# Spectrum sums on GpSimd beside VectorE products that read PSUM, with third buffers and an earlier start of loads and transposes

## The chip, the cores and the metric

One core of a Trainium2 chip. The metric is the device time of the whole kernel in microseconds (us). Most executions of one kernel agree within 0.3%, so differences below about 0.5 us are read with care. "Span" is the profiled time from the first to the last instruction, 1.8 us less than the timed run of the same execution (211.5 of 213.35 us for before).

## The reference, cut to what matters

```python
def _A_ref(x, w_r, w_i):                       # x: (1, 2048, 640) bf16
    X = rfft2(x.astype(float32))
    X = X * (w_r + 1j * w_i)                   # the filter: w_r, w_i (2048, 321)
    return irfft2(X, s=(2048, 640)).astype(bfloat16)

def _B_ref(x, w_gate, w_up, w_down):           # (640,1536), (640,1536), (1536,640)
    return ((x @ w_gate) * (x @ w_up)) @ w_down

xn = layernorm(x)
out = x + _A_ref(xn, w_r, w_i) + _B_ref(xn, w_gate, w_up, w_down)
```

The two branches share the normalised input. The Fourier branch is done as matmuls with small tables and radix-5 butterflies on VectorE. In the middle it has 16 filter steps. Each takes a part of the spectrum from PSUM, multiplies it by the weights, and forms sums of the products. These sums are what the change moves.

## The kernel before

The kernel gives every piece of work to a list scheduler of its own, written in Python, as a task with an engine, an assumed duration, the buffers it reads and writes, and a priority. The scheduler fixes one order for each engine before the kernel is built. Each engine's queue is written in that order. So a change of a duration, of a buffer or of an engine re-plans everything that comes after it.

The loads at the start and the statistics of the normalisation:

```python
dma("ld_sm", V("SM"), d_sm.rearrange("p t n -> p (t n)"), 128 * 768, [(b_sm, None)], prio=0.002, q="act")
# ... (cut)
for gi, (b0, nb) in enumerate(_X_LOADS):
    dma("ld_x%d" % gi, v_x[:, b0:b0 + nb, :], xv[:, b0:b0 + nb, :], 128 * nb * 1280,
        [(b_x, ("s", b0, b0 + nb))], prio=(0.0, 0.01, 0.02, 0.03, 0.042, 0.06)[gi])
# ... (cut) for each row block b below 8:
def em_bn(c, b=b):
    c.e.bn_stats(v_st[:, b, 0:6], v_x[:, b, 0:320])
    return c.e.bn_stats(v_st[:, b, 6:12], v_x[:, b, 320:640])
T("bn%d" % b, "dve", 800.0, em_bn, reads=[(b_x, ("s", b, b + 1))], writes=[(b_st, ("b", b, b + 1))], prio=pbase)
```

Row blocks 0 to 3 of the normalised x are transposed on TensorE (tasks `T0_b`), the others by DMA transposes on the queue of SyncE (L816). Then follow the gate/up units (`GU_ft_b`, L951: TensorE, evicted by ScalarE at L709, multiplied on VectorE at L966).

A filter step:

```python
for t in range(16):
    r2 = t % 2
    # ... (cut: four loads of filter rows; D: matmuls, L994; C: matmuls into a pair of PSUM banks, L1015-L1018)
    def em_wm(c, tc=tc, r2=r2, wr=wr):         # products: PSUM times weights in SBUF
        for h in range(2):
            for w in range(2):
                c.e.tensor_tensor(v_p[:, r2, w, :, 128*h:128*h+128], xh, wv[:, w], _OP.mult)    # L1030, cut
        return c.e.tensor_tensor(v_p[:, r2, :, :, 256:321], ps[:, bk:bk + 2, 256:321], ...)     # L1033, cut
    def em_cb(c, r2=r2):                       # sums: two SBUF inputs each
        p00, p01, p10, p11 = (v_p[:, r2, 0, 0], v_p[:, r2, 0, 1], v_p[:, r2, 1, 0], v_p[:, r2, 1, 1])
        c.e.tensor_tensor(v_y[:, r2, 512:768], p01[:, 0:256], p10[:, 0:256], _OP.add)           # L1045
        c.e.scalar_tensor_tensor(v_y[:, r2, 896:961], p01[:, 256:321], -1.0, p10[:, 256:321], _OP.mult,
                                 _OP.subtract)                                                  # L1046
        c.e.tensor_tensor(v_y[:, r2, 768:833], p00[:, 256:321], p11[:, 256:321], _OP.subtract)  # L1048
        return c.e.tensor_tensor(v_y[:, r2, 256:512], p00[:, 0:256], p11[:, 0:256], _OP.subtract)  # L1049
    T("CB_%d" % t, "dve", 2 * _d_dve(256) + 2 * _d_dve(65), em_cb, ...)
    # ... (cut: NG on ScalarE copies and negates, L1054-L1056; IA: inverse matmuls, L1070/L1071)
```

After it come the inverse stage (matmuls L1099, butterflies on VectorE L1121 to L1154) and the down-projection (L1172 and L1180), whose result is added by VectorE (L1187).

Of the kernel before, what the change touches and what calls it, by code (L numbers as in the profile page):

```python
# [15 lines left out]
_DMA_LAT = 1000.0  # L16
_DMA_ISSUE = 440.0
# [489 lines left out]
_LP = 321  # L507
_SN = math.sin(2.0 * math.pi / 5.0)
# [4 lines left out]
def _d_mm(n):  # L513
    return max(n, 64) / 2.4 + 2.5


def _d_dve(n):
    return n * 1.04 + 65.0


def _d_dve_psum(n):
    return n * 1.04 + 70.0
# [14 lines left out]
def _d_act(n):  # L537
    return n * 0.833 + 80.0
# [8 lines left out]
def _build(nc, A_x, A_w_r, A_w_i, B_w_gate, B_w_up, B_w_down, out, opts=None):  # L547
# [3 lines left out]
    with es:  # L551
# [8 lines left out]
        sch.caps = {"glu": opts.get("cap_glu", 2), "acc": opts.get("cap_acc", 4), "fill": 1}  # L560
        lay = {}
# [43 lines left out]
        b_p = alloc("P", 2 * 4 * 2 * _LP)  # L605
        b_y = alloc("Y", 2 * 1024)
        o_end = max(o_end, cur[0])
        cur[0] = o_3
        b_tc = alloc("TC", 2 * 2560)
        b_vt = alloc("VT", 2 * 2048)  # L610
# [12 lines left out]
        def V(name):  # L623
            off, sz = lay[name]
            return arena[:, off: off + sz]
# [29 lines left out]
        v_p = V("P").bitcast(_F32).rearrange("p (r w c l) -> p r w c l", r=2, w=2, c=2)  # L655
        v_y = V("Y").rearrange("p (r n) -> p r n", r=2)
        v_tc = V("TC").bitcast(_F32).rearrange("p (r s u n) -> p r s u n", r=2, s=5, u=2)
# [54 lines left out]
        dma("ld_sm", V("SM"), d_sm.rearrange("p t n -> p (t n)"), 128 * 768, [(b_sm, None)], prio=0.002, q="act")  # L712
# [34 lines left out]
        for gi, (b0, nb) in enumerate(_X_LOADS):  # L747
            dma("ld_x%d" % gi, v_x[:, b0:b0 + nb, :], xv[:, b0:b0 + nb, :], 128 * nb * 1280,
                [(b_x, ("s", b0, b0 + nb))], prio=(0.0, 0.01, 0.02, 0.03, 0.042, 0.06)[gi])
        muls = {}  # L750
        for gi, (b0, nb) in enumerate(_LN_GROUPS):
            pbase = 1.0 + 0.05 * gi if gi < 4 else opts.get("ln_prio", 5.99) + 0.05 * (gi - opts.get("ln_lead", 3))
            for b in range(b0, b0 + nb):
# [13 lines left out]
                else:  # L767
                    def em_bn(c, b=b):
                        c.e.bn_stats(v_st[:, b, 0:6], v_x[:, b, 0:320])  # L769
                        return c.e.bn_stats(v_st[:, b, 6:12], v_x[:, b, 320:640])  # L770
                    T("bn%d" % b, "dve", 800.0, em_bn, reads=[(b_x, ("s", b, b + 1))],
                      writes=[(b_st, ("b", b, b + 1))], prio=pbase)
# [3 lines left out]
                    T("ag%d" % b, "dve", 130.0, em_ag, reads=[(b_st, ("b", b, b + 1))],  # L776
                      writes=[(b_mv, ("b", b, b + 1))], prio=pbase)
            if b0 >= opts.get("act_stats", 8):
# [3 lines left out]
                T("mb%d" % b0, "dve", 160.0, em_mb, reads=[(b_m32, ("b", b0, b0 + nb)), (b_ss, ("b", b0, b0 + nb))],  # L782
# [6 lines left out]
            T("ve_%d" % gi, "dve", 80.0, em_ve, reads=[(b_mv, gk)], writes=[(b_ve, gk)], prio=pbase - 0.006)  # L789
# [3 lines left out]
            T("sd_%d" % gi, "act", 120.0, em_sd, reads=[(b_ve, gk)], writes=[(b_sd, gk)], prio=pbase - 0.006)  # L793
# [3 lines left out]
            T("rs_%d" % gi, "dve", 80.0, em_rs, reads=[(b_sd, gk)], writes=[(b_rs, gk)], prio=pbase)  # L797

            for b in range(b0, b0 + nb):
# [4 lines left out]
                T("sub%d" % b, "dve", 290.0, em_sub, reads=[(b_mv, ("b", b, b + 1))],  # L804
# [6 lines left out]
                muls[b] = T("mul%d" % b, ("dve", "act") if b >= 4 else "dve", {"dve": 290.0, "act": _d_act(640) + 93}, em_mul, reads=[(b_rs, ("b", b, b + 1))],  # L811
                  writes=[(b_x, ("s", b, b + 1))], prio=pb)

                if b >= opts.get("xt_dma", 4):
                    def em_xt(c, b=b):
                        return c.e.dma_start_transpose(v_xt[:, :, b * 128:(b + 1) * 128], v_x[:, b, :])  # L816
                    T("xt%d" % b, "sp", opts.get("xt_issue", 1500.0), em_xt, reads=[(b_x, ("s", b, b + 1))],
# [13 lines left out]
                t0 = T("T0_%d" % b, "pe", 5 * _d_mm(128), em_t0, reads=[(b_x, ("s", b, b + 1)), (b_sm, None)],  # L831
                       prio=pb, bank="pair" if b < opts.get("e0_split", 2) else "single", cls="a")

                if b < opts.get("e0_split", 2):
# [9 lines left out]
                    hold(t0, es_)  # L844
                    continue
# [10 lines left out]
        for g in range(8):  # L856
# [46 lines left out]
            for u in range(2):  # L903
                def em_r(c, gr=gr, u=u):
                    bk = bank_of(c.t)
                    ins = None
                    for k, (f, o) in enumerate(((0, 1), (1, 0), (1, 1), (0, 0), (2, 0))):
# [8 lines left out]
                       reads=[(b_f, ("r", 3 * gr, 3 * gr + 3)), (b_sm, None)], prio=pf, bank="pair", cls="a")  # L916
# [19 lines left out]
        for ui, (at_, ci, ft0) in enumerate(units):  # L936
# [6 lines left out]
            for u in range(2):  # L943
# [10 lines left out]
                gu = T("GU_%d_%d" % (ft, b0), "pe", 10 * _d_mm(n), em_gu,  # L954
# [322 lines left out]
```

## Time and profile before

| | before |
|---|---|
| time, median of 4 runs beside the changed kernel | 212.87 us (212.59 to 213.29) |
| span | 211.5 us |
| VectorE busy | 185.1 us |
| GpSimd busy | 0.2 us |
| first transpose on TensorE | 5.88 us |
| matmuls that start late | 8.2 us |

All matmuls from the first transpose on, back to back, would take 194.6 us. What the distances between their starts exceed that by is summed by stretch of the span and called **late matmuls**. First transpose + 194.6 + late matmuls + 2.7 for the last output gives the span.

### The profile page before, as it was taken

Reading aid. Unit: us, or ns where it says so; the run is one execution under the profiler, and the core shown is the slowest. Engines: PE = TensorE matmul, PEld = TensorE weight load, DVE = VectorE, ACT = ScalarE, POOL = GpSimd, SP = SyncE. Lnnn points to the kernel's source line nnn. Section 1 sums busy time; section 2 is a strip of 40 time slices with the busy share of each in tenths; the row PEclk is TensorE's granted clock in tenths of the full one; section 3 lists DMA queues with packets and bytes.
Section 4 is the critical chain, followed back from the end, with each engine's and each line's share of the span. In section 5 each row is a group of like instructions: output and inputs, shape, how many; then the busy total and the mean of one; then the engine's idle time right before and its main releaser. Section 6 shows DMA issues by size and latency. Waiting matters only on the chain.

```text
span 211.5 us, 5204 instructions
## 1 busy us (share of the span) xinstructions
PE 202.6 (96%) x2044; PEld 169.4 (80%) x2044; DVE 185.1 (87%) x536; ACT 122.1 (58%) x281; POOL 0.2 (0%) x4
## 2 busy tenths in 40 slices
PE   8799999799999999989999999999999899999994
PEld 7699899688898998978888898898766677667773
DVE  3699989899999989389999999948999999999821
ACT  2375899799866666878999897776222202200000
POOL 0000000000000000000000000000000000000000
PEclk9999999999999999999999999999999999999999
DMA  6999999531133000002224233025042223222411
GB/s 190 304 341 395 384 299 218 104 62 31 34 64 65 0 3 0 0 18 56 56 58 120 55 62 90 3 62 155 3 121 82 64 63 108 81 77 65 126 47 47
DMA packets 30456, 21.74 MB, mean 103 GB/s; under 512 B 10336, under 2 KB 29408, under 8 KB 30304
## 3 DMA queue, kind: packets, MB, share of 16 engines
q1 hardware_dynamic: 28320, 20.34, 35.6%
q10 hardware_dynamic: 2112, 1.08, 1.9%
q8 instruction: 16, 0.26, 0.5%
q14 instruction: 8, 0.07, 0.1%
HBM read 16.82 MB, written 2.62 MB: 92 GB/s over the span
## 4 chain that ended last, share of the span: by engine, by line
PE 67%; DVE 22%; DMA 6%; issue 3%; ACT 1%; SPq 0%; DVEq 0%
PE ps L951 41%; PE ps L1172 12%; DMA arena<-arena 3%; DMA arena<-in_A_x_dram 2%; PE ps L1070 2%; PE ps L1071 2%; DVE arena L1187 2%; PE ps L994 2%; PE ps L912 2%; DVE arena L1144 1%; DVE arena L1145 1%; DVE arena L1153 1%; DVE arena L1137 1%; PE ps L1015 1%; ACT arena L709 1%
## 5 line engine op out<-in xcount | busy, mean ns | idle before, releaser
L709 ACT ACTIVATE arena<-ps 128x512 bf16<-128x512 f32 (+5 forms) x189 | 99.9, 572 | 55.0 <-PE ps L1099 28.2
L951 PE MATMUL ps<-arena 128*128 128x256 bf16 (+1 forms) x1080 | 112.8, 261 | 2.8 <-DMA arena<-arena 1.2
L951 PEld LDWEIGHTS ps<-arena 128*128 128x128 bf16 x1080 | 93.6, 98 | 14.2 <-ACT arena L709 1.6
L1172 PE MATMUL ps<-arena 128*128 128x320 bf16 x384 | 56.5, 299 | 0.3 <-DVE arena L1187 0.3
L1172 PEld LDWEIGHTS ps<-arena 128*128 128x128 bf16 x384 | 37.2, 98 | 14.7 <-DVE arena L1187 0.7
L966 DVE TENSOR_TENSOR arena<-arena 128x512 bf16<-128x512 bf16 (+1 forms) x54 | 21.1, 390 | 10.5 <-ACT arena L709 10.4
L1030 DVE TENSOR_TENSOR arena<-ps,arena 128x256 f32<-128x256 f32 x64 | 22.6, 414 | 0.0
L1187 DVE TENSOR_TENSOR arena<-ps,arena 128x320 bf16<-128x320 f32 x32 | 15.4, 482 | 6.7 <-PE ps L1180 6.7
L1071 PE MATMUL ps<-arena 128*128 128x128 bf16 x80 | 10.7, 219 | 0.0
L1070 PE MATMUL ps<-arena 128*128 128x128 bf16 x80 | 10.6, 219 | 0.0
L1180 PE MATMUL ps<-arena 128*128 128x320 bf16 x32 | 9.1, 300 | 0.5 <-DVE arena L1154 0.4
L1070 PEld LDWEIGHTS ps<-arena 128*128 128x128 bf16 x80 | 8.7, 112 | 0.5
L865 DVE TENSOR_TENSOR arena<-arena 128x384 f32<-128x384 bf16 x16 | 8.8, 550 | 0.0
L1071 PEld LDWEIGHTS ps<-arena 128*128 128x128 bf16 x80 | 8.7, 112 | 0.1
L769 DVE BATCH_NORM_STATS2 arena<-arena 128x6 f32<-128x320 bf16 x8 | 3.9, 489 | 3.8 <-DMA arena<-in_A_x_dram 3.7
L1033 DVE TENSOR_TENSOR arena<-ps,arena 128x260 f32<-128x260 f32 x16 | 7.1, 441 | 0.0
L1045 DVE TENSOR_TENSOR arena<-arena 128x256 bf16<-128x256 f32 x16 | 6.7, 421 | 0.2
L1054 ACT ACTIVATE arena<-arena 128x256 bf16<-128x256 bf16 x16 | 6.6, 414 | 0.3 <-DVE arena L1049 0.2
L1049 DVE TENSOR_TENSOR arena<-arena 128x256 bf16<-128x256 f32 x16 | 6.7, 418 | 0.0
L866 DVE TENSOR_TENSOR arena<-arena 128x256 f32<-128x256 bf16 x16 | 6.7, 417 | 0.0
L1152 DVE TENSOR_TENSOR arena<-arena 128x640 bf16<-128x640 f32 x8 | 6.5, 818 | 0.1
L762 ACT ACTIVATE arena<-arena 128x640 bf16<-128x640 bf16 x8 | 6.6, 828 | 0.0
(71 smaller groups left out, 212.2 us busy)
## 6 DMA issues: line engine op xcount, KB each, us to landing
arena<-in_A_x_dram SPq DMA_DIRECT2D x20, 160.0 KB, 2.6
out_dram<-arena SPq DMA_DIRECT2D x32, 80.0 KB, 1.6
arena<-c_tf SPq DMA_DIRECT2D x4, 384.0 KB, 11.8
arena<-in_A_w_r_dram SPq DMA_DIRECT2D x32, 40.1 KB, 2.4
arena<-in_A_w_i_dram SPq DMA_DIRECT2D x32, 40.1 KB, 2.2
arena<-in_B_w_gate_dram SPq DMA_DIRECT2D x4, 320.0 KB, 7.9
arena<-in_A_x_dram SPq DMA_DIRECT2D x1, 1280.0 KB, 12.1
arena<-c_ti SPq DMA_DIRECT2D x2, 512.0 KB, 14.5
```

What stands on the lines that cost most here:

```text
L709: return c.e.activation(dst, src, _ACTF.Copy)
L865: c.e.tensor_tensor(uo[:, o, :, 0:3, :], v_xb[:, b:b + 2, 0:6:2, :], v_xb[:, b:b + 2, 5:10:2, :], op)
L866: ins = c.e.tensor_tensor(uo[:, o, :, 3:5, :], v_xb[:, b:b + 2, 6:10:2, :], v_xb[:, b:b + 2, 1:5:2, :], op)
L951: ins = c.e.matmul(ps[:, bk, w * n:(w + 1) * n], v_gw[:, w, j, ft, :], v_xt[:, j, rows], start=(j == 0), stop=(j == 4))
L966: return c.e.tensor_tensor(v_ht[:, ft0:ft0 + 2, rows], v_gbf[:, rr, :, 0:n], v_gbf[:, rr, :, n:2 * n], _OP.mult)
L1030: c.e.tensor_tensor(v_p[:, r2, w, :, 128 * h:128 * h + 128].rearrange("p c (m k) -> p c m k", k=4), xh.rearrange("p c (m k) -> p c m k", k ...
L1033: ins = c.e.tensor_tensor(v_p[:, r2, :, :, 256:321], ps[:, bk:bk + 2, 256:321].unsqueeze(1).to_broadcast([128, 2, 2, 65]), v_w[:, wr, :, 0 ...
L1070: c.e.matmul(dst, l1, v_ti[:, t, 0, :], start=True, stop=False)
L1071: ins = c.e.matmul(dst, l2, v_ti[:, t, 1, :], start=False, stop=True)
L1172: ins = c.e.matmul(ps[:, bk, 0:320], v_ht[:, ft, a * 128:(a + 1) * 128], v_wd[:, ft, sl3], start=(ft == 7), stop=False)
L1180: return c.e.matmul(ps[:, bank_of(ag2), 0:320], v_sm[:, 2, :], v_v[:, a, sl3], start=False, stop=True)
L1187: return c.e.tensor_tensor(v_out[:, a % 2, sl3], ps[:, bk, 0:320], v_xr[:, xs, sl3], _OP.add)
```

## The change

The intent: VectorE is full in the filter stage and busy for 87% of the span, GpSimd idle. The products read PSUM, to which GpSimd has no access by the page that the prediction cites, so they stay on VectorE, and the two long sums of each step go to GpSimd. The two short sums stay on VectorE. Third buffers are to hide the longer latency. Independently of that, the start and the order of the loads are changed, the scheduler's assumed durations are set anew, and at most two tasks of class `a`, those of the spectrum among them, may hold PSUM banks at once (the cap). The core of the diff:

```diff
-_DMA_LAT = 1000.0
-_DMA_ISSUE = 440.0
+_DMA_LAT = 1300.0
+_DMA_ISSUE = 520.0
 def _d_dve(n):
-    return n * 1.04 + 65.0
+    return n * 1.04 + 72.0
 # (cut: the other durations likewise, e.g. DMA transposes 1500 -> 1100)
         sch.caps = {"glu": ..., "acc": ..., "fill": 1}
+        if opts.get("cap_a", 2):
+            sch.caps["a"] = opts.get("cap_a", 2)
-        b_p = alloc("P", 2 * 4 * 2 * _LP)
-        b_y = alloc("Y", 2 * 1024)
+        b_p = alloc("P", 3 * 4 * 2 * _LP)
+        b_y = alloc("Y", 2 * _YS)
+        b_y3 = alloc("Y3", _YS, at=lay["STAT"][0])
+        b_tc3 = alloc("TC3", 2560, at=lay["GBF"][0])
-        dma("ld_sm", V("SM"), ..., prio=0.002, q="act")
+        dma("ld_sm0", v_sm[:, 0, :], ..., prio=0.002, q="act")
+        dma("ld_sm1", v_sm[:, 1:3, :], ..., prio=0.25)
-                [(b_x, ("s", b0, b0 + nb))], prio=(0.0, 0.01, 0.02, 0.03, 0.042, 0.06)[gi])
+                [(b_x, ("s", b0, b0 + nb))], prio=(0.0, 0.003, 0.02, 0.03, 0.042, 0.06)[gi])
-                    T("bn%d" % b, "dve", 800.0, em_bn, ...)          # both halves in one task
+                        bns.append(T("bn%d_%d" % (b, i), "dve", 420.0, em_bn, ...))
+                    if b == 1:
+                        bns[0].deps.add(muls[0])
+                        bns[1].deps.add(e0_first)                     # behind the first copy from PSUM
-                        64 * 642, ..., after=[wpad])                   # filter rows
+                        64 * 642, ..., after=[wpad, muls[opts.get("w_after", 15)]])
 # (cut: the same "after" for the inverse tables and the down weights)
-            def em_cb(c, r2=r2):
+            def em_cb(c, ar=ar):
+                c.e.tensor_tensor(v_y[ar][:, 512:768], p01[:, 0:256], p10[:, 0:256], _OP.add)
+                return c.e.tensor_tensor(v_y[ar][:, 256:512], p00[:, 0:256], p11[:, 0:256], _OP.subtract)
+            ce = opts.get("cb_eng", "pool")
+            T("CB_%d" % t, ce, {"dve": 2 * _d_dve(256), "pool": opts.get("cb_pool", 1600.0)}, em_cb, ...)
+            def em_cd(c, ar=ar):
                 # (the two sums of 65 columns, as before)
+            T("CD_%d" % t, "dve", 2 * _d_dve(65), em_cd, ...)
-        sch.affinity = opts.get("affinity", 600.0)
+        sch.affinity = opts.get("affinity", 1500.0)
```

## The prediction

> **What bounds the kernel now.** I read the page first, then the sum of waits, then the timeline of TensorE, VectorE and the DMA queue where the waits point, then the windows by stage.
>
> ```profile
> span 211.5 us, 5204 instructions
> PE 202.6 (96%) x2044; PEld 169.4 (80%) x2044; DVE 185.1 (87%) x536; ACT 122.1 (58%) x281; POOL 0.2 (0%) x4
> ...
> PE   8799999799999999989999999999999899999994
> DVE  3699989899999989389999999948999999999821
> ```
>
> TensorE is busy for 96% of the span, VectorE for 87%, and GpSimd does nothing. Busy TensorE is not proof of a full pace, so I summed in the trace the distances between the starts of successive matmuls. Back to back, a matmul of 128 columns takes 55.9 ns, of 256 columns 109, of 320 columns 135.7, of 321 columns 137. The first transpose starts at 5.88 us; all matmuls from there, back to back, would take 194.6 us; the output after the last one takes 2.7 us. That makes 5.9 + 194.6 + 2.7 = 203.2 of the 211.5 us. The other **8.2 us** are matmuls that started late, and they are all that this change can win: it removes no matmul. The lost time by place: 1.3 us before 10 us, 0.8 from 10 to 30, 1.5 from 30 to 40, 1.0 from 40 to 55, 0.8 at 91.6, 2.75 between 157 and 189. From 60 to 90 and from 93 to 155 nothing is lost.
>
> The three places that matter, as the timeline shows them:
>
> ```profile
> 8.16 1.05 PE L951 MATMUL ps<-arena 128*128 128x128 bf16 x16 [0.95 <-DVE arena L775]
> ...
> 6.87 0.49 DVE L769 BATCH_NORM_STATS2 arena<-arena 128x6 f32<-128x320 bf16 x1 [1.14 <-DMA arena<-in_A_x_dram]
> 7.28 0.48 DVE L770 BATCH_NORM_STATS2 arena<-arena 128x6 f32<-128x320 bf16 x1
> 7.68 0.34 DVE L710 COPY arena<-ps 128x384 bf16<-128x384 bf16 x1
> ...
> 39.07 6.91 PE L951 MATMUL ps<-arena 128*128 128x256 bf16 x60 [1.21 <-DMA arena<-arena]
> ...
> 32.16 7.94 SPq L816 DMA_TRANSPOSE arena<-arena  x4
> ...
> 158.11 0.45 PE L1180 MATMUL ps<-arena 128*128 128x320 bf16 x2 [0.41 <-DVE arena L1154]
> 160.61 0.72 PE L1099 MATMUL ps<-arena 128*128 128x128 bf16 x10 [0.29 <-DVE arena L1131]
> ```
>
> At 8.16 us the first gate matmuls start: their transposed input sat in PSUM from about 6.3 us, but VectorE waited for the second row block of x (landed at 6.85), did both its statistics, and only then the copy. At 39.07 TensorE waits for DMA transposes whose input was normalised by 25.7 us; they were issued from 32.16 on, because sixteen filter loads and others, at 0.6 us of queue each, stood before them. After 157 us TensorE waits for VectorE's last butterflies (L1121 to L1154).
>
> ```profile
> 105.02 0.41 DVE L1045 TENSOR_TENSOR arena<-arena 128x256 bf16<-128x256 f32 x1
> 105.35 0.22 DVE L1046 SCALAR_TENSOR_TENSOR arena<-arena 128x65 bf16<-128x65 f32 x1
> 105.49 0.22 DVE L1048 TENSOR_TENSOR arena<-arena 128x65 bf16<-128x65 f32 x1
> 105.62 0.42 DVE L1049 TENSOR_TENSOR arena<-arena 128x256 bf16<-128x256 f32 x1
> 105.96 1.41 DVE L1030 TENSOR_TENSOR arena<-ps,arena 128x256 f32<-128x256 f32 x4
> ...
> 92.00:138.00 46.00, 45.56 (x503) 40.26 (x504) 45.16 (x149) 39.90 (x109) 0.00 (x0) 1.00 0.25 59
> ```
>
> This is one of the 16 filter steps, and the window over them all (TensorE, its weight loads, VectorE, ScalarE, GpSimd): VectorE is full (45.2 of 46 us), yet TensorE loses only 0.6 us, since gate/up matmuls fill its time. So VectorE sets the pace of the filter steps, but not the time there; it sets when the last butterflies can begin.
>
> **What the Trainium skill says.** "GPSIMD Engine Reference", 4.1 Engine selection, says that GpSimd has no access to PSUM: hence the products stay on VectorE. The same page, 3.1 Elementwise, gives 4497 ns for a two-input add of 2048 fp32 elements, about 2.6 cycles each: for 256 elements, an estimate of 0.56 us, 0.65 us with dispatch. No run here shows it yet; VectorE's cost is measured, 0.335 us from start to start. "SBUF — State Buffer", Who interferes with whom, says that a VectorE instruction with two SBUF inputs contends with a GpSimd instruction that reads SBUF (whoever is first holds the pair for its whole instruction), and that one with at most one SBUF input does not. The products (L1030, L1033) read PSUM and one SBUF operand, so they should run free; the two short sums that stay on VectorE and the gate products (L966) can be blocked. With GpSimd idle the trace of before cannot confirm it. "Perfetto Trace Analysis", Optimizing Scalar/DVE Operations, warns that offloading between these two engines might not help for this reason.
>
> **The change part by part.**
> 1. *Sums to GpSimd.* VectorE loses L1045 and L1049: 2 x 0.335 = 0.67 us per step, 10.7 us in 16 steps. A step now takes 48.2/16 = 3.01 us (91.2 to 139.4). Left: products 1.77, short sums 0.27, about 0.2 of gate product per step: 2.25 to 2.35 us. GpSimd needs about 1.3 us per step, less than that, and starts when the products of its step are done, so it runs mostly beside the next products. But ScalarE is next: 39.9 of 46 us in this window, 2.6 us per step, of which about 0.5 falls away with every gate eviction that moves to later. Balanced, I put a step at 2.6 to 2.7 us, so the filter stage ends some 5 to 6 us earlier, and about as much gate/up work is left to lie beside the first butterflies. By itself this frees no TensorE time in the stage, where almost none is lost.
> 2. *Third buffers* for products, sums and the butterfly input. The sums' longer latency (some 0.8 us more per step) is hidden by the first two. The third butterfly input lies on the gate buffer, so it is usable only after the last gate unit; two pairs go before that, as now. With 5 us more of lead the butterflies (6.7 us a pair with the output adds, against 7.6 us of TensorE work a pair: 48 x 0.136 + 4 x 0.136 + 10 x 0.056) should stay ahead. Of the 2.75 us lost there I count **2.2** as won.
> 3. *Second row block of x loaded ahead of the gate weights; statistics split around the first copy.* The copy can follow the transposes at about 6.4 us. The gate weights landed at 5.33 and 6.28 us and now come some 0.5 us later, about 6.8. The gate matmuls start at 7.0 to 7.4 instead of 8.16: **0.9** of 1.1 us.
> 4. *Filter, inverse-table and down-weight loads only after the last normalisation* (66.4 us). The transposes go out when their blocks are ready, some 6 us earlier: **1.4** us won at 38 us. The delayed loads need about 20 x 0.6 = 12 us of queue, done by about 81 us; the products first use them at 91 us.
> 5. *Scheduling constants and the cap on PSUM pairs* change the static order. The 0.75 us at 91.6, where three spectrum tasks held the pairs, should mostly go: **0.5**.
> 6. *Against it:* contention of VectorE with GpSimd, and a fixed order planned with 1.6 us of GpSimd per step: I take **0.8** us of new TensorE waits.
>
> Sum: 2.2 + 0.9 + 1.4 + 0.5 - 0.8 = 4.2 us from these terms; a few tenths more of the waits between 40 and 55 us, which hang on late gate evictions, bring it to **4.8** us. The timed runs have 212.7 us, so the prediction is about **207.9 us**.
>
> **The rivals.**
> - *The GpSimd sums block VectorE.* If every step costs VectorE one whole GpSimd instruction (0.65 us), the 0.67 us won per step is gone; the order, planned for faster steps, leaves TensorE waiting, up to 0.3 us x 16 = 5 us. Then items 3 and 4 alone remain: 210 to 212 us. For it speaks that the short sums start with the GpSimd sums of the same step; against it, that the products, three quarters of VectorE's work, read PSUM.
> - *ScalarE becomes the bound of the filter stage.* It is already at 87% there. Then a step takes 2.8 us or more, the lead is 3 us, and still covers the 2.75 us: 208 to 209 us.
> - *VectorE still bounds the end of the first stage.* Its forward butterflies end at 84.8 us whatever the transposes do; earlier matmuls then only use up gate work sooner. That takes nothing back as long as gate work lasts, as it did (to 146 us). If not, the 2.3 us of items 3 and 4 turn into waits later: 209 to 210 us.
> - *Everything fits:* hardly 2 us of late matmuls remain: 206 us.
>
> **Range and chances.** The floor is 203.2 + 1.2 (timed run less span) = 204.4 us; no such order here gets below 1.5 us of waits, so the low end is 205.8. The high end is the blocking rival in a mild form, 210.8. Two per cent is 208.45 us, close above my middle: faster by over 2% 0.58, within 2% 0.39, slower 0.03 (waits of several microseconds at every step would be needed).
>
> **What would show it.** Right, if in the profile after: GpSimd has 32 sums of about 0.65 us; products still last about 0.41 us each; the wait for DMA transposes near 38 us is gone; gate matmuls start before 7.5 us; the products' steps are 2.6 to 2.7 us apart; and waits of L1180 and L1099 on VectorE nearly vanish. Wrong, if VectorE's short sums or gate products are stretched or preceded by gaps of 0.3 us or more, if TensorE shows new waits at the filter steps for ScalarE or GpSimd, or if the new order brings waits in places that had none.

## More of the kernel before

The line of the short sums and of the gate product, which the argument turns on, in the groups of before (line, engine, operation, out<-in, count; busy us, mean ns; idle just before):

```profile
L966 DVE TENSOR_TENSOR arena<-arena 128x512 bf16<-128x512 bf16 (+1 forms) x54 | 21.1, 390 | 10.5 <-ACT arena L709 10.4
L1046 DVE SCALAR_TENSOR_TENSOR arena<-arena 128x65 bf16<-128x65 f32 x16 | 3.5, 221 | 0.0
L1048 DVE TENSOR_TENSOR arena<-arena 128x65 bf16<-128x65 f32 x16 | 3.5, 221 | 0.0
```

A sum of 65 columns takes 221 ns, a gate product 390 ns on the mean of its two shapes.

## The result, and the profile after

**215.41 us** median of 4 runs (215.3 to 215.59), against 212.87: ratio 1.0118, 95% interval 1.0098 to 1.0138. Slower by 1.2%, where 2.3% faster was predicted. A ratio here is always the mean time of one kernel's fast runs over that of the other's fast runs of the same rounds, so it isn't quite the ratio of the medians quoted.

The page of after, its span and its busy time by engine:

```profile
span 213.8 us, 5221 instructions
...
PE 202.4 (95%) x2044; PEld 169.7 (79%) x2044; DVE 185.9 (87%) x504; ACT 122.2 (57%) x281; POOL 22.6 (11%) x36
```

GpSimd works 22.6 us, as intended. VectorE issues 32 instructions fewer, yet is busy for 185.9 us against 185.1. The sums that left took 32 x 0.335 = 10.7 us. Something gave all of it back. The groups show what (line numbers have moved: L1068 and L1070 are the short sums, L981 is the gate product, L1045 and L1048 the products):

```profile
L981 DVE TENSOR_TENSOR arena<-arena 128x512 bf16<-128x512 bf16 (+1 forms) x54 | 22.6, 419 | 12.1 <-ACT arena L717 11.9
L1045 DVE TENSOR_TENSOR arena<-ps,arena 128x256 f32<-128x256 f32 x64 | 22.5, 410 | 0.0
L1061 POOL TENSOR_TENSOR arena<-arena 128x256 bf16<-128x256 f32 x16 | 11.7, 729 | 0.0
L1060 POOL TENSOR_TENSOR arena<-arena 128x256 bf16<-128x256 f32 x16 | 11.3, 709 | 119.3 <-DVE arena L1048 117.4 <-PE ps L966 1.8
L1070 DVE TENSOR_TENSOR arena<-arena 128x65 bf16<-128x65 f32 x16 | 11.3, 705 | 0.0
L1068 DVE SCALAR_TENSOR_TENSOR arena<-arena 128x65 bf16<-128x65 f32 x16 | 6.3, 393 | 0.3
```

The products, which read PSUM and one SBUF operand, keep their 410 ns. The two short sums rise from 221 ns each to 393 and 705: 16 x (172 + 484) ns = 10.5 us. The gate products add 54 x 29 ns = 1.6 us. A wait of this kind doesn't stand in the column of idle time. It looks like a long instruction. The timeline of VectorE, then of GpSimd, in two steps shows it directly:

```profile
91.89 0.23 DVE L1068 SCALAR_TENSOR_TENSOR arena<-arena 128x65 bf16<-128x65 f32 x1
92.04 0.66 DVE L1070 TENSOR_TENSOR arena<-arena 128x65 bf16<-128x65 f32 x1
...
94.65 0.66 DVE L1068 SCALAR_TENSOR_TENSOR arena<-arena 128x65 bf16<-128x65 f32 x1
95.23 0.77 DVE L1070 TENSOR_TENSOR arena<-arena 128x65 bf16<-128x65 f32 x1
```

```profile
91.94 0.68 POOL L1060 TENSOR_TENSOR arena<-arena 128x256 bf16<-128x256 f32 x1 [91.50 <-DVE arena L1048]
92.58 0.73 POOL L1061 TENSOR_TENSOR arena<-arena 128x256 bf16<-128x256 f32 x1
94.46 0.76 POOL L1060 TENSOR_TENSOR arena<-arena 128x256 bf16<-128x256 f32 x1 [1.15 <-DVE arena L1048]
95.18 0.72 POOL L1061 TENSOR_TENSOR arena<-arena 128x256 bf16<-128x256 f32 x1
```

In the first step GpSimd's sum runs from 91.94 to 92.62. The second short sum starts at 92.04 and ends at 92.70, just after it. In the next step the gate product delays VectorE, and each short sum ends about 0.1 us after a GpSimd sum (95.31 after 95.22, 96.00 after 95.90). Both engines get the same start signal, the end of the products, so they meet in every step: the second short sum takes 661 ns or more in all 16 steps, the first one 657 ns or more in six and 228 to 233 ns in the other ten.

Where TensorE lost time, by stretch (late matmuls, us; the stage names are rough):

| stretch | before | after |
|---|---|---|
| first matmul after the warm-up | 5.88 | 5.00 |
| to 30 us: start | 2.1 | 4.1 |
| 30 to 55: transposes | 2.4 | 0.3 |
| 88 to 138: filter steps | 0.9 | 5.5 |
| 138 to 146 | 0.0 | 0.5 |
| 146 to the end: inverse stage | 2.7 | 0.9 |
| sum, with 55 to 88 us | 8.2 | 11.3 |

In before the first matmul is the first transpose. In after two fillers come at 5.00 and the transpose at 5.50. +3.1 of late matmuls and -0.9 of start give the +2.3 us of the span. Two stretches improve by some 2 us each. The filter steps lose 4.6 us, and the start loses as well. The timeline of TensorE at both places in after:

```profile
7.22 1.29 PE L966 MATMUL ps<-arena 128*128 128x128 bf16 x20 [0.51 <-DMA arena<-in_B_w_gate_dram]
9.70 1.29 PE L966 MATMUL ps<-arena 128*128 128x128 bf16 x20 [1.19 <-DMA arena<-in_B_w_gate_dram]
10.83 0.44 PE L841 MATMUL ps<-arena 128*128 128x128 bf16 x5
...
101.01 0.45 PE L1009 MATMUL ps<-arena 128*128 128x128 bf16 x5 [1.09 <-DVE arena L1048]
...
118.92 1.27 PE L966 MATMUL ps<-arena 128*128 128x256 bf16 x10 [1.56 <-DVE arena L1048]
```

At 101.0 and 118.9 us TensorE waits for the products (L1048), which stand behind the short sums in VectorE's queue. At the start the gate units begin at 7.22 instead of 8.16, as predicted. But then two more gate units stand ahead of the second row block's transposes (L841) and wait for weights that land at 9.65 us. Before, those transposes ran at 9.28.

The DMA queue, for the transposes that the late loads were to free:

```profile
27.77 18.03 SPq L829 DMA_TRANSPOSE arena<-arena  x6
```

They go out at 27.77 us instead of 32.16, and the wait of TensorE at 39 us is gone.

### The profile page after: what moved, and what is told of

Its sections match the earlier page's. It is cut to its first block, busy times and chain, and to the rows that moved or that the text cites. A ratio compares the mean times of both kernels' runs of the same rounds, so it can differ in the third digit from the quotient of the medians.

```text
span 213.8 us, 5221 instructions
## 1 busy us (share of the span) xinstructions
PE 202.4 (95%) x2044; PEld 169.7 (79%) x2044; DVE 185.9 (87%) x504; ACT 122.2 (57%) x281; POOL 22.6 (11%) x36
## 4 chain that ended last, share of the span: by engine, by line
PE 63%; DVE 20%; SPq 6%; DMA 5%; ACT 3%; issue 1%; POOL 1%; DVEq 0%; ACTq 0%
PE ps L966 33%; PE ps L1195 22%; DVE arena L1045 9%; SPq L711 6%; DMA arena<-c_sm 5%; DVE arena L1070 3%; DVE arena L1048 2%; ACT arena L717 2%; PE ps L927 2%; PE ps L1120 2%; PE ps L1203 2%; DVE arena L1068 2%; DVE arena L981 1%; PE ps L1091 1%; PE ps L1009 1%
## 5 line engine op out<-in xcount | busy, mean ns | idle before, releaser
L966 PEld LDWEIGHTS ps<-arena 128*128 128x128 bf16 x1080 | 93.7, 98 | 15.1 <-DMA arena<-in_B_w_gate_dram 2.0
L1195 PEld LDWEIGHTS ps<-arena 128*128 128x128 bf16 x384 | 37.4, 98 | 14.1
L981 DVE TENSOR_TENSOR arena<-arena 128x512 bf16<-128x512 bf16 (+1 forms) x54 | 22.6, 419 | 12.1 <-ACT arena L717 11.9
L1060 POOL TENSOR_TENSOR arena<-arena 128x256 bf16<-128x256 f32 x16 | 11.3, 709 | 119.3 <-DVE arena L1048 117.4
L1045 DVE TENSOR_TENSOR arena<-ps,arena 128x256 f32<-128x256 f32 x64 | 22.5, 410 | 0.0
L1061 POOL TENSOR_TENSOR arena<-arena 128x256 bf16<-128x256 f32 x16 | 11.7, 729 | 0.0
L1091 PE MATMUL ps<-arena 128*128 128x128 bf16 x80 | 10.7, 219 | 0.8 <-ACT arena L1077 0.3
L1070 DVE TENSOR_TENSOR arena<-arena 128x65 bf16<-128x65 f32 x16 | 11.3, 705 | 0.0
L1092 PE MATMUL ps<-arena 128*128 128x128 bf16 x80 | 10.7, 219 | 0.0
L1091 PEld LDWEIGHTS ps<-arena 128*128 128x128 bf16 x80 | 8.7, 112 | 1.9 <-ACT arena L1077 0.8
L780 DVE BATCH_NORM_STATS2 arena<-arena 128x6 f32<-128x320 bf16 x16 | 7.2, 479 | 3.3 <-DMA arena<-in_A_x_dram 3.1
L1092 PEld LDWEIGHTS ps<-arena 128*128 128x128 bf16 x80 | 8.7, 112 | 0.0
L1009 PE MATMUL ps<-arena 128*128 128x128 bf16 (+1 forms) x80 | 6.8, 219 | 2.0 <-DVE arena L1048 2.0
L1009 PEld LDWEIGHTS ps<-arena 128*128 128x128 bf16 x80 | 5.4, 97 | 3.3 <-DVE arena L1048 2.6
L1075 ACT ACTIVATE arena<-arena 128x256 bf16<-128x256 bf16 x16 | 6.6, 413 | 1.2 <-POOL arena L1061 0.9
L1048 DVE TENSOR_TENSOR arena<-ps,arena 128x260 f32<-128x260 f32 x16 | 6.9, 431 | 0.0
```

The lines of the kernel that those rows point to most:

```text
L966: ins = c.e.matmul(ps[:, bk, w * n:(w + 1) * n], v_gw[:, w, j, ft, :], v_xt[:, j, rows], start=(j == 0), stop=(j == 4))
L981: return c.e.tensor_tensor(v_ht[:, ft0:ft0 + 2, rows], v_gbf[:, rr, :, 0:n], v_gbf[:, rr, :, n:2 * n], _OP.mult)
L1009: ins = c.e.matmul(psflat[:, bk * 512 + k * 128: bk * 512 + k * 128 + n], v_uq[:, k, t, :], v_fd[:, k * 128: k * 128 + n], start=True, sto ...
L1045: c.e.tensor_tensor(v_p[:, ar, w, :, 128 * h:128 * h + 128].rearrange("p c (m k) -> p c m k", k=4), xh.rearrange("p c (m k) -> p c m k", k ...
L1070: return c.e.tensor_tensor(v_y[ar][:, 768:833], p00[:, 256:321], p11[:, 256:321], _OP.subtract)
L1091: c.e.matmul(dst, l1, v_ti[:, t, 0, :], start=True, stop=False)
```

## The experiments

The theory: a GpSimd sum with two SBUF inputs holds the read path that a VectorE instruction with two SBUF inputs needs, and this costs the filter stage more than the moved sums save. The main rival: the new order, constants and buffers cost the time, and contention is a minor part. Every edit of a task re-plans the order, so I compared the order in which the matmuls ran in each pair of traces. It is the same in a_memset and after (all 2044 matmuls), and in b_late and before. In the other runs the planner was at work too.

### 1. The same order without GpSimd reading SBUF (a_memset)

```diff
-                c.e.tensor_tensor(v_y[ar][:, 512:768], p01[:, 0:256], p10[:, 0:256], _OP.add)
-                return c.e.tensor_tensor(v_y[ar][:, 256:512], p00[:, 0:256], p11[:, 0:256], _OP.subtract)
+                c.e.memset(v_y[ar][:, 512:768], 0.0)
+                c.e.memset(v_junk[:, 0:256], 0.0)
+                c.e.memset(v_y[ar][:, 256:512], 0.0)
+                return c.e.memset(v_junk[:, 256:512], 0.0)
```

GpSimd still works in each step, from the same event on (16.87 / 16 = 1.05 us a step, in the window below, where two sums take 1.37 in the timeline of after), with the same waits before and after, but it only writes. Its output is wrong, which doesn't matter for the time.

> The changed kernel in the very same order, with each GpSimd sum replaced by two memsets (one into the sum's place, one into a spare buffer) that read no SBUF; the result is wrong on purpose. Theory 1 (VectorE instructions with two SBUF inputs stand still while a GpSimd instruction that reads SBUF runs): the short sums fall from 0.39 and 0.70 us to 0.22 each, the gate products from 0.458 to 0.42, VectorE busy from 185.9 to about 175 us, late matmuls between 88 and 146 us from 6.0 to under 2 us, time 210.5 to 212.5 us. Rival 2 (the new order itself or the three-buffer pipeline is at fault): the short sums fall, but at least 4 us of late matmuls stay there, time 214 us or more. Rival 3 (GpSimd's writes are what blocks): the short sums stay at 0.39 and 0.70, time 215.

Measured: 209.71 us, ratio 0.9851 (0.9836 to 0.9865). From the groups of this run (L1073 and L1075 are the short sums, L984 the gate product):

```profile
L984 DVE TENSOR_TENSOR arena<-arena 128x512 bf16<-128x512 bf16 (+1 forms) x54 | 20.9, 389 | 17.6 <-ACT arena L720 17.3
L1064 POOL MEMSET arena<- 128x256 f32 x16 | 5.0, 311 | 0.0
...
L1073 DVE SCALAR_TENSOR_TENSOR arena<-arena 128x65 bf16<-128x65 f32 x16 | 3.6, 227 | 0.3
L1075 DVE TENSOR_TENSOR arena<-arena 128x65 bf16<-128x65 f32 x16 | 3.6, 222 | 0.0
```

That is below the range expected. Short sums back at 227 and 222 ns, gate products at 389. VectorE is busy for 174.4 us, exactly the 10.7 us less that was hoped for. The window over the filter steps, first after, then this run (busy us of TensorE, weight loads, VectorE, ScalarE, GpSimd):

```profile
88.00:138.00 50.00, 46.00 (x493) 39.29 (x490) 45.35 (x116) 39.87 (x107) 19.55 (x28) 1.00 0.24 54
```

```profile
88.00:138.00 50.00, 50.00 (x552) 44.34 (x550) 38.45 (x127) 43.54 (x120) 16.87 (x64) 1.00 0.27 61
```

Late matmuls there fall from 5.5 to 0.3 us. So with the same order the contention costs **5.7 us** of run time (215.41 to 209.71). A small part can be that memsets are done 0.3 us sooner than the sums. In a_cdfirst, below, real sums start later still, and more than half of the time comes back all the same.

### 2. The sums back on VectorE (a_dve), or held until the short sums are done (a_cdfirst)

```diff
 # a_dve
-            ce = opts.get("cb_eng", "pool")
+            ce = opts.get("cb_eng", "dve")
 # a_cdfirst: CB is created behind CD, and waits for it
-            T("CD_%d" % t, "dve", 2 * _d_dve(65), em_cd,
+            cd = T("CD_%d" % t, "dve", 2 * _d_dve(65), em_cd,
+            T("CB_%d" % t, ce, {...}, em_cb, ..., prio=pq - 0.001, after=[cd])
```

> The changed kernel with the 256-wide sums back on VectorE, all else kept (the order is planned anew). Theory 1: the sums' 10.7 us on VectorE replace about 10.6 us of standing still, so VectorE's busy time stays at 184 to 187 us and the time at 214 to 216.5 us. Rival 2 (the sums' way over GpSimd costs by its latency): the time falls to 212 us or less.

> The changed kernel with one dependence more: GpSimd's sums of a step wait for VectorE's two short sums of the same step. Theory 1: the short sums fall to about 0.22 us each, GpSimd then runs beside products that read PSUM; only gate products that fall into its 1.4 us can be blocked; VectorE busy 176 to 180 us, time 211.5 to 213.5 us. Rival 2: with GpSimd 0.3 us later per step it gets no faster, 215 us or more.

a_dve: 214.93 us, ratio 1.0091 (1.0069 to 1.0113). No contention, but the rest of the change, with VectorE doing all its old work, is slower than before: late matmuls of 5.9 us after 138 us. Half of the main rival is right: the new order isn't good by itself (experiment 6).

a_cdfirst: 212.08 us, ratio 0.9951 (0.9922 to 0.998). Real sums, on GpSimd, meeting products instead of short sums. VectorE and GpSimd in the same two steps:

```profile
92.23 0.22 DVE L1066 TENSOR_TENSOR arena<-arena 128x65 bf16<-128x65 f32 x1
92.37 1.41 DVE L1045 TENSOR_TENSOR arena<-ps,arena 128x256 f32<-128x256 f32 x4
```

```profile
92.54 0.64 POOL L1060 TENSOR_TENSOR arena<-arena 128x256 bf16<-128x256 f32 x1 [92.10 <-DVE arena L1066]
93.13 0.73 POOL L1061 TENSOR_TENSOR arena<-arena 128x256 bf16<-128x256 f32 x1
```

The four products take 1.41 us with two GpSimd sums beside them, as they take alone. That is the clean half of the prediction: VectorE with one operand in PSUM runs free. VectorE's busy time is 175.9 us. The order is planned anew here, and it has one wait of 1.7 us for a filter load (TensorE, 129.8 us), so this run isn't at its best. Still, 3.3 of the 5.7 us are back although GpSimd starts later.

### 3. All four sums on GpSimd (a_allpool)

If a short sum must wait for GpSimd, it may as well be done there. ScalarE makes the negated copy that the `scalar_tensor_tensor` used to make.

```diff
-                c.e.scalar_tensor_tensor(v_y[ar][:, 896:961], p01[:, 256:321], -1.0, p10[:, 256:321], _OP.mult,
-                                         _OP.subtract)
+                c.e.tensor_tensor(v_y[ar][:, 1024:1089], p01[:, 256:321], p10[:, 256:321], _OP.add)
-            T("CD_%d" % t, "dve", 2 * _d_dve(65), em_cd,
+            T("CD_%d" % t, "pool", 550.0, em_cd,
-                c.e.activation(v_y[ar][:, 833:896], v_y[ar][:, 897:960], _ACTF.Copy, scale=-1.0)
+                c.e.activation(v_y[ar][:, 833:896], v_y[ar][:, 1025:1088], _ACTF.Copy)
+                c.e.activation(v_y[ar][:, 896:961], v_y[ar][:, 1024:1089], _ACTF.Copy, scale=-1.0)
```

> The changed kernel with the two short sums on GpSimd too (as plain adds; ScalarE makes the negated copy, 65 wide in place of 63). Theory 1: VectorE has no two-SBUF-input instruction of its own left in a filter step but the gate product; VectorE busy 171 to 176 us, GpSimd about 1.9 us per step, time 211 to 213.5 us. Rival 2: GpSimd's longer chain per step (0.5 us more) makes the inverse matmuls wait, 215 us or more.

Measured: 210.49 us, ratio 0.9887 (0.987 to 0.9903), correct, and below the range expected. Three of GpSimd's four groups (the other long sum, L1061, takes 742 ns):

```profile
L1060 POOL TENSOR_TENSOR arena<-arena 128x256 bf16<-128x256 f32 x16 | 10.6, 660 | 103.5 <-DVE arena L1048 103.4
L1069 POOL TENSOR_TENSOR arena<-arena 128x65 bf16<-128x65 f32 x16 | 6.1, 378 | 0.0
L1068 POOL TENSOR_TENSOR arena<-arena 128x65 bf16<-128x65 f32 x16 | 5.2, 325 | 0.0
```

2.1 us of GpSimd in a step of 2.75 us, VectorE at 171.9 us, late matmuls of 0.6 us in the filter steps. Only the gate product (407 ns against 389) still meets GpSimd. With real sums 4.9 us of the 5.7 are back. This isn't contention alone: the order is planned anew, and the short sums' own 0.28 us a step have left VectorE too. Together with a_cdfirst it speaks against the memsets' speed as the main cause of the gain.

### 4. Parts of the change alone in the kernel before

b_late holds the filter, inverse-table and down-weight loads back until the last normalisation and changes only SyncE's queue. b_pool moves the two long sums to GpSimd, with two buffers. b_late_allpool has late loads and all four sums on GpSimd. b_start has the new start alone: the lines for `ld_sm`, `ld_x` and `bn` of the diff above.

```diff
 # b_late (and the same for the inverse tables and the down weights)
-                        semkey=("w", wr), after=[wpad])
+                        semkey=("w", wr), after=[wpad, muls[15]])
 # b_pool
+                c.e.tensor_tensor(v_y[:, r2, 512:768], p01[:, 0:256], p10[:, 0:256], _OP.add)
+                return c.e.tensor_tensor(v_y[:, r2, 256:512], p00[:, 0:256], p11[:, 0:256], _OP.subtract)
+            T("CB_%d" % t, "pool", 1600.0, em_cb, ...)     # short sums: a task of their own on "dve"
```

> The kernel before with one part of the change: the filter, inverse-table and down-weight loads wait for the last normalisation, so the DMA transposes go ahead of them. Theory: the 1.4 us wait of TensorE for the transposes at 38 us is gone and nothing takes its place: 210.9 to 212.0 us. Rival (VectorE's forward butterflies set the end of that stage anyway, or the late loads come late for the filter steps): 212.5 us or more.

> The kernel before with the 256-wide sums alone moved to GpSimd (two buffers, old start, old loads). Theory 1 (standing still takes back what leaves VectorE): short sums 0.35 to 0.75 us, VectorE busy 183 to 187 us, 212.5 to 215.5 us, no gain over before. Rival (the loss came from the rest of the change): VectorE busy under 180 us, 211.5 us or less.

> The kernel before with the late loads and with all four sums of a step on GpSimd (two buffers, old start, old scheduling constants). Theory 1: VectorE busy 170 to 174 us; with the transposes' 1.4 us and the last butterflies' 2 us won and the old start kept, 207.5 to 209.5 us, less than the changed kernel with all sums on GpSimd (210.5), by the 1.2 us that the new start loses. Rival (the third buffers and new constants are needed for GpSimd's longer chain): 210.5 us or more.

> The kernel before with the new start alone (x block 1 loaded ahead of the gate weights, the statistics split so that each half waits for its own load, the small constants loaded in two pieces); sums, buffers, filter and late loads as before. Its planned order becomes GU_0, GU_1, GU_2, GU_3, T0_1, as in the changed kernel. The prediction on record says the start gains 0.9 us: then about 212.2 us, late matmuls before 30 us from 2.1 to about 1.2 us. The theory from the trace of after says it loses: GU_2 and GU_3 stand ahead of T0_1 in TensorE's queue and wait for the second piece of gate weights, which lands at 9.7 us; then late matmuls before 30 us grow to 3 to 4 us, first real matmul near 5.0 us, and the time is 213.0 to 214.5 us (ratio 1.000 to 1.006).

| run | us | ratio (95%) | late matmuls: to 30 / 30-55 / 88-138 / 138 on |
|---|---|---|---|
| before (batch of b_late) | 213.1 | 1 | 2.1 / 2.4 / 0.9 / 2.8 |
| b_late | 212.33 | 0.9958 (0.9937, 0.9979) | 2.3 / 1.5 / 0.9 / 2.8 |
| b_pool | 217.75 | 1.0214 (1.0197, 1.0232) | 1.9 / 2.0 / 6.7 / 1.8 |
| b_late_allpool | 212.16 | 0.9955 (0.9929, 0.9981) | 2.0 / 1.4 / 1.6 / 2.1 |
| b_start | 211.63 | 0.9938 (0.9924, 0.9953) | 2.6 / 1.4 / 0.9 / 1.3 |

b_pool repeats the contention without anything else of the change: +4.7 us, over 2 us above the range that I expected, with short sums of 284 and 681 ns and 6.7 us of late matmuls in the filter steps. b_late wins 0.8 us, not the 1.4 predicted, and lies between its two expectations. My reading, not tested: the order of TensorE, VectorE and ScalarE was planned with the late transposes in mind and can't use the early ones fully. b_late_allpool ended 2.7 us above its expected range.

b_start contradicts what I had read from the trace of after. The same queue order is in it, its start is 0.7 us worse (first transpose 6.14 us, late matmuls before 30 us 2.6), and still the kernel is 1.4 us faster. Its filter steps begin at 88.7 us instead of 91.2, and the waits between 30 and 55 us and in the inverse stage shrink. As I read it, a loss at the start isn't a loss of the kernel as long as VectorE gets ahead.

### 5. The start in the changed order: four tries

With all sums on GpSimd (210.49 us), p_order puts T0_1 ahead of the gate units that wait for weights. p_bw280_o2 does the same with the statistics of the third row block behind T0_1's copy. p_bw250 leaves the order to the planner with a lower assumed bandwidth. m_oldstart is a_memset with the start of before (wrong).

```diff
 # p_order, p_bw280_o2
+        for ft in range(2, 12):
+            gus[(ft, 0)].deps.add(gus[(1, 1)])
 # p_bw280_o2 also
+                    if b == 2:
+                        bns[0].deps.add(e0_second)
 # p_bw280_o2 and p_bw250
-        sch.dma_bw = float(opts.get("dma_bw", 330.0))
+        sch.dma_bw = float(opts.get("dma_bw", 280.0))      # p_bw250: 250.0
 # m_oldstart: the lines for ld_sm, ld_x and bns[..].deps of the diff above, undone in a_memset
```

> The changed kernel with all sums on GpSimd (210.5 us), and with the gate units of the first row block that need the second weight piece placed behind the transposes and the first two gate units of the second row block. Theory (the new start loses because these units stand in TensorE's queue and wait for weights that land at 9.65 us, while the second row block's transposes could run): late matmuls before 30 us fall from 3.5 to about 2.2 us, time 208.8 to 209.8 us. Rival (the start is bound by the arrival of weights however it is ordered): 210.2 to 211 us.

> The version with all sums on GpSimd (210.5 us, ratio 0.989, start loss 3.5 us), with the bandwidth that the kernel's own planner assumes for loads lowered from 330 to 250, so that its plan no longer puts gate units ahead of the weights they wait for: GU_0, GU_1, T0_1, GU_2, GU_3, with T0_1's copy ahead of the statistics of x block 2. If the planned order is the start's loss: start loss 2.1 to 2.6 us, the rest unchanged, 209.0 to 209.8 us (ratio 0.981 to 0.985). If the loss is elsewhere (the loads themselves land later than planned and something waits for them in any order): start loss stays at 3.5 us, 210.2 to 210.8 us (ratio 0.987 to 0.990).

> The version with all sums on GpSimd, with the order of gate units and T0_1 set by hand and the statistics of x block 2 put behind T0_1's copy (the wait of 1.8 us that the first try at a new order ran into), planner bandwidth 280. If the queue order of both TensorE and VectorE is the start's loss: start loss 2.1 to 2.6 us and 209.0 to 209.8 us (ratio 0.981 to 0.985), like the run with bandwidth 250. If the loss is not in the order: 210.2 to 211.0 us (ratio 0.987 to 0.991).

> The changed kernel with the sums replaced by memsets (209.71 us, 3.9 us of late matmuls before 30 us; result wrong on purpose), with the start of before: x block 1 behind the first gate weights, its statistics not held back, the small constants in one load. If the new start costs the changed kernel time: late matmuls before 30 us about 2.1 us and 208.2 to 209.0 us (ratio 0.978 to 0.982). If it pays, as it did alone in the kernel before (211.6 us against 213.1): 210.6 to 211.4 us (ratio 0.989 to 0.993).

| run | us | ratio (95%) | first matmul + late matmuls to 30 us | late from 138 us |
|---|---|---|---|---|
| a_allpool | 210.49 | 0.9887 (0.987, 0.9903) | 9.2 | 0.9 |
| p_order | 211.12 | 0.9914 (0.9879, 0.9949) | 9.4 | 0.9 |
| p_bw280_o2 | 210.71 | 0.9899 (0.9875, 0.9922) | 8.2 | 0.9 |
| p_bw250 | 211.64 | 0.994 (0.9924, 0.9957) | 7.5 | 3.0 |
| a_memset | 209.71 | 0.9851 (0.9836, 0.9865) | 9.3 | 0.9 |
| m_oldstart | 210.08 | 0.987 (0.9856, 0.9885) | 8.9 | 1.6 |

The start itself can be mended: p_bw250 reaches 7.5 us where before has 8.0 and after 9.1. None of the tries made the kernel faster, since late matmuls came back elsewhere. And with the old start the changed kernel is no faster: the new start pays 0.4 us there by the medians, though the two intervals overlap. The expectations that a mended or an old start would bring 1 us or so all fell. p_bw280_o2 came within the range of its rival (the loss isn't in the order). p_order and p_bw250 were slower than either range, and m_oldstart lies between its two. The late matmuls of the start are real, but gate units done later make up for them or don't, depending on the order.

### 6. Third buffers, and the constants

m_2buf is a_memset with two product, sum and butterfly buffers (wrong). p_2buf is a_allpool with two. b_const is the kernel before with the new constants and the cap, b_cap with the cap alone. b_start_late_allpool adds the parts that won.

```diff
 # m_2buf, p_2buf (and ar -> t % 2 in the tasks of products, sums and NG, IA)
-            by, y0 = (b_y, 3 * ar) if ar < 2 else (b_y3, 0)
+            by, y0 = b_y, 3 * (t % 2)
-            gt = (a // 2) % 3
+            gt = (a // 2) % 2
 # b_cap; b_const has also every changed duration of the diff
+        sch.caps["a"] = 2
```

> The changed kernel with the sums on GpSimd replaced by memsets (209.71 us; result wrong on purpose) and with two product, sum and butterfly buffers instead of three. The prediction's step: third buffers are what wins the 2 us of late matmuls between 146 and 189 us; then that loss rises from 0.87 to 2.5 us or more and the time to 211.0 us or more (ratio 0.991 or above). Rival: the loss there depends on the fixed order and on how far the filter stage is ahead, not on the buffers; then 0.8 to 1.6 us of loss and 209.4 to 210.2 us (ratio 0.983 to 0.987).

> The version with all four sums on GpSimd and ScalarE making the negated copy (210.49 us, ratio 0.989), with two product, sum and butterfly buffers. The run with memsets and two buffers showed third buffers to win nothing there (209.65 against 209.71 us). If that holds with real sums: 209.8 to 211.0 us (ratio 0.985 to 0.991). If the real sums' longer latency needs the third buffer: waits on GpSimd in the filter stage, 211.5 us or more (ratio 0.993 or above).

> The kernel before with the scheduling constants and the cap on PSUM pairs of the changed kernel alone; every instruction as before, only their order planned anew. The prediction's item 5 says this wins 0.5 us (the late matmuls at 91.6 us): 212.2 to 212.6 us. Rival: with VectorE still making the sums, the new order leaves VectorE without a lead at the end of the filter stage, as in the changed kernel with its sums put back on VectorE (5.9 us of late matmuls after 138 us); then 214 to 217 us (ratio 1.006 to 1.02).

> The kernel before with the cap of two PSUM pairs for spectrum work alone, constants as before; its plan ends at 208.8 us on the planner's own clock, against 209.3 for before and 217.1 for the run with the new constants and the cap (which took 217.8 us). If the cap is what the prediction's item 5 took it for: the 0.8 us of late matmuls near 91.6 us go, 212.0 to 212.8 us (ratio 0.995 to 0.999). If it was the cap that made that run slow: a filter stage over 50 us long, 214 us or more (ratio above 1.005).

> The kernel before with the new start, the late loads and all four sums on GpSimd (no operation with two SBUF inputs left on VectorE in the filter steps beside the gate product), two buffers, constants of before. Alone: start 211.6, late loads and sums 212.2 us against 213.0. If the parts add: 210.6 to 211.0 us (ratio 0.988 to 0.991). If the new start's lead on VectorE and the sums' relief win the same waits: 211.3 to 212.0 us (ratio 0.992 to 0.995).

| run | us | ratio (95%) | late matmuls 88-138 / 138-146 / 146 on |
|---|---|---|---|
| a_memset, three buffers | 209.71 | 0.9851 (0.9836, 0.9865) | 0.3 / 0.0 / 0.9 |
| m_2buf | 209.65 | 0.9845 (0.9828, 0.9861) | 0.7 / 0.0 / 0.7 |
| a_allpool, three buffers | 210.49 | 0.9887 (0.987, 0.9903) | 0.6 / 0.0 / 0.9 |
| p_2buf, 5 rounds | 210.16 | 0.9858 (0.9836, 0.988) | 0.6 / 0.1 / 0.7 |
| b_const | 217.77 | 1.021 (1.0177, 1.0242) | 0.0 / 4.1 / 5.1 |
| b_cap | 212.61 | 0.9977 (0.9958, 0.9995) | 0.0 / 1.5 / 1.8 |
| b_start_late_allpool | 212.84 | 0.9997 (0.9982, 1.0012) | 1.6 / 0.0 / 1.6 |

Third buffers win nothing in these pairs, with memsets or with real sums, each order planned for its buffers. The fall of late matmuls in the inverse stage comes from the order. Which feature of the order does it isn't settled by these runs.

b_const is the clearest miss of the prediction's item 5: 4.7 us slower, not 0.5 faster, and slower than the range that I had given its rival. TensorE loses nothing in the filter steps, but these are 3.4 us apart instead of 3.0, and after 142 us the gate work is used up and TensorE waits for the last steps. The timeline of TensorE there, and the windows over it:

```profile
144.51 0.25 PE L1071 MATMUL ps<-arena 128*128 128x128 bf16 x1 [1.73 <-ACT arena L1057]
147.25 0.30 PE L1071 MATMUL ps<-arena 128*128 128x128 bf16 x1 [1.99 <-ACT arena L1057]
```

```profile
145.00:148.00 3.00, 1.01 (x13) 0.84 (x11) 1.42 (x6) 1.41 (x4) 0.00 (x0) 0.65 0.39 109
148.00:150.00 2.00, 1.11 (x12) 0.88 (x11) 0.00 (x0) 0.70 (x1) 0.00 (x0) 0.50 0.18 41
```

The column behind the five engines is the granted clock. In finer windows it falls to 0.50 at 145.9 us, some 0.65 us into the second of two waits of nearly 2 us, and matmuls of 128 columns follow each other at 107 ns instead of 56. This adds to the loss, and all four runs of b_const have it (clock 0.984 or 0.992 over the span). With the cap alone (b_cap) the wait at 91.6 us goes and the kernel is 0.3 us faster, though the steps stretch too (3.3 us apart) and the late matmuls after 138 us grow from 2.8 to 3.3. So the cap alone doesn't cost 4.7 us: that comes only with the new constants, which were run together with the cap. a_dve has the same cap and constants, and steps 3.4 us apart.

b_start_late_allpool missed both its ranges: parts that win 1.4 and 0.9 us each add up to nothing (212.84 against 212.80 us in its batch). With two buffers and the old constants its late matmuls are 8.4 us, as many as before.

The best correct version is p_2buf: 210.16 us, ratio 0.9858 (0.9836 to 0.988), 1.4% faster than the kernel before and 2.4% by the medians than the changed one.

## Why the prediction was wrong

**Item 6, contention of VectorE with GpSimd, is the step that failed.** It put 0.8 us against the change. With the order unchanged it measures 5.7 us of run time (a_memset), and 10.5 + 1.6 us of VectorE standing still. The facts were all in the prediction: the Trainium skill's "SBUF — State Buffer", Who interferes with whom, says that whoever is first holds the shared path for its whole instruction, and the prediction named the two short sums and the gate products as those that can be blocked. What failed is the overlap and with it the weight. Item 1 lets GpSimd run "mostly beside the next products", and against the rival the prediction sets that three quarters of VectorE's work reads PSUM: a share of the work, not the time at which it runs. The 0.8 itself has no working. In fact the short sums are released by the same event as the GpSimd sums. At least one short sum meets one in every step, and an instruction of 221 ns waits for one of 709. The rival "The GpSimd sums block VectorE" had the size right: one GpSimd instruction per step (0.65 us; measured 656 ns on the short sums, in part by luck, as this is the mean of ten steps that lose some 0.45 us and six that lose 0.98) and up to 5 us of TensorE waits (4.6 more than before). The prediction left it outside the middle. It put that rival at 210 to 212 us since it let items 3 and 4 stand beside it.

**Item 1, sums to GpSimd:** right on the relief (10.7 us, exactly, in a_memset) and on the products (410 ns). The step was put at 2.6 to 2.7 us. Without contention it is 2.8 (a_memset), 2.75 (a_allpool) or 2.7 (a_cdfirst), with it 3.25, from the first product of the first step to that of the last, over 15. GpSimd's sums take 709 and 729 ns, 0.64 and 0.73 where nothing is in their way (a_cdfirst), near the 0.65 estimated.

**Item 2, third buffers, 2.2 us:** the 1.9 us were won, but not by the buffers. m_2buf and p_2buf have as little late work in that stretch with two, in orders of their own. Right in size, by luck, and wrong in cause.

**Item 3, the start, 0.9 us won:** the gate units do start 0.9 us sooner. But first matmul and late matmuls to 30 us together grow from 8.0 to 9.1 us, as two gate units wait for weights ahead of T0_1. The trace of before could have told: its second piece of gate weights lands at 9.67 us, and only two gate units can run without it (the 6.28 us that the prediction takes for gate weights is the landing of the first up weights). The sum of late matmuls isn't the total, though: alone the new start wins 1.4 us (b_start), in the changed order 0.4 (m_oldstart against a_memset).

**Item 4, late loads, 1.4 us:** the stretch won 2.1 in the changed kernel. The loads alone, with the old order, win 0.8 of run time and 0.9 in this stretch (b_late), and the new start alone brings the stretch down as far (b_start). What the rest needs isn't shown. Direction right, and the wait at 39 us is gone as predicted.

**Item 5, constants and cap, 0.5 us:** the wait at 91.6 us goes (0.9 to 0.3 us in that stretch without contention, 0.0 in b_cap). The prediction looked only there. With VectorE's old work the constants and the cap together cost 4.7 us (b_const). My reading is that they suit a kernel in which the sums cost VectorE nothing (a_memset, 209.7 us), and that the contention made them cost it all the same.

The floor of 204.4 us takes 1.2 us between run and span, which compares different executions. Within one it is 1.8, so the floor is 205.0.

Of the four rivals, ScalarE as the bound didn't come about: it is busy for 43.5 of 50 us in the filter steps of a_memset, and TensorE loses 0.3 us.

By stretch, from before to after: start +1.1 (with the earlier first matmul), 30 to 55 us -2.1, filter steps +4.6, to 146 us +0.5, inverse stage -1.9: together +2.2 of the 2.3 us of the span. The run without contention had left 5.4 us of late matmuls and 209.7 us, inside the predicted range but still 1.8 us above its middle: the start, expected 0.9 us better and measured 1.3 us worse there, accounts for it by stretch. What stays open is whether p_2buf is slower than m_2buf (0.5 us by the medians, 0.3 by the ratios, whose intervals overlap), what each changed duration costs, and which feature of the order sets the inverse stage.

## What to carry to other kernels

Before moving work with two SBUF operands to GpSimd, list which VectorE instructions with two SBUF operands are released by the same event: each can wait for a whole GpSimd instruction (here in every step), and the profile shows it as a longer instruction, not as idle time. Move those along, or order them first, rather than weigh them by their share. In a kernel with a planned static order, test a suspected cost with the order held fixed (here a memset in place of the sum): parts tried one by one, each with its own plan, didn't add up, as 1.4 and 0.9 us won alone made nothing together.

## What the Trainium skill lacked or had wrong

- "SBUF — State Buffer", Who interferes with whom, is borne out on every point that the runs touch. VectorE with one operand in PSUM runs free beside GpSimd sums (410 ns), VectorE with two SBUF operands waits (221 to 393 and 705 ns), and a GpSimd instruction that only writes SBUF doesn't hold it (227 and 222 ns beside memsets of 311 ns). It doesn't say that the profiler books the wait as busy time of the instruction, here 12 us of VectorE's 185.9.
- "GPSIMD Engine Reference", 3.1 Elementwise, gives cycles per element and only a large two-input case. Small sums carry a fixed part that it has no figure for: 256 columns took 640 to 742 ns and 65 columns 302 to 378 ns. From the 640 and 325 ns, an estimate of 1.65 ns per column and 0.22 us fixed.
- "Perfetto Trace Analysis", Optimizing Scalar/DVE Operations, warns that moving work between VectorE and GpSimd might not help. Here it cost 4.7 us alone (b_pool), and with all four sums moved and the rest of the change the kernel was 2.4 us faster than before (a_allpool, 210.49 against 212.94 us in its batch). The page has no such case.
- "TensorE: Matmul & The Clock Gate", What's actually happening, says that the clock halves after at least one idle window of about 3.4 us. It has no figure for how much of such a window must be idle; further down it tells of short pauses that do it, without their lengths. Here the clock fell to 0.50 after a wait of 1.73 us, 10 matmuls in 0.75 us and some 0.65 us of the next wait, and 128-column matmuls came 107 ns apart (b_const). In a_dve it fell after a wait of 1.69 us, 10 matmuls and 0.3 us. Waits of 1.09 and 1.56 us in after, 18 us apart, left the clock at 1.00.
